# RWKV-6 attention with a SERF feed-forward: level six beside the state's products, and the last factor of the keys a step ahead

## The chip, the cores and the metric

The kernel runs on one core of one Trainium2 chip. The metric is the device time of one execution in microseconds (us). Five engines with their own queues work beside each other and meet by semaphores: TensorE (PE; its weight loads are shown apart as PEld), VectorE (DVE), ScalarE (ACT), GpSimd (POOL) and SyncE (SP), whose queue here only starts DMA transfers. All data is float32.

## The reference, cut to what matters

Attention with a decaying state, 4 batches, 8 heads, 768 tokens, head size 48; then a feed-forward on 3072 tokens (384 to 2048 to 384):

```python
for t in range(S):
    cur = einsum('bhd,bhe->bhde', u * k_t, v_t)
    y[:, :, t] = einsum('bhd,bhde->bhe', r_t, state + cur)
    state = w_t[..., None] * state + einsum('bhd,bhe->bhde', k_t, v_t)

h = x @ w_in
sp = maximum(h, 0.0) + log1p(exp(-abs(h)))     # softplus
g = h * erf(sp)
out = g @ w_out
```

`x` is `y` with heads and head size joined. The recurrence runs along the tokens, so the kernel can't treat them all at once.

## The kernel before, in words

**Steps.** The tokens are cut into chunks of 128, each into two halves of 64. A step is one chunk of a pair of batches, with all 8 heads: 12 steps, 0 to 11. Within a half, r and k are multiplied level by level with products of decays (levels one to six, blocks of 2 to 64 tokens), and small products of r and k give the attention inside the half (`own`). Across halves the state carries over (`middle` is the state between the two halves of a chunk, `S` before, `S_next` after).

**Late steps.** Steps 5 to 11 are written by `attend_late`. They take the nearest 16 tokens in another way: VectorE and GpSimd multiply rows of r, k and decays for each distance 1 to 15 (`term`, L463 and L467), VectorE sums them (L453), and the sums go through DRAM and back (`by_blocks`, `by_tokens`) to become the next step's `own` (L514). This preparation of step s + 1 is a generator, `prepare`, run in pieces (`next(following)`, the token F) inside step s. The same generator multiplies k by its decays in place; the result goes to DRAM (`k_blocks`, L499) and comes back with the tokens on the partitions as `kT` (L509). `kT` still lacks the decay over whole blocks of 16: `spread_blocks` turns `over_blocks` by two small products with the identity (L672), copies them (`few`, L678), sends them out (`g_rows`, L683) and fetches them repeated (`spread`, L688); VectorE multiplies `kT` by `spread` (L718). Products of `kT` and v give the state's increment (`state_part`, L659).

**Small products on TensorE.** All of these use 48 or 64 rows, and four or so at once in parts of the array: `from_own` (L584, own times v, into `y`), `level_products` (L552), `through_state` (L610, r times state), `state_part` (L659), the spread products (L672). Between them stand the large products of the feed-forward, 128 by 128.

**The feed-forward, by tokens.** A table, `LATE` and `USUAL`, says what is done in the seven stages of a late step. P is a piece of the projection of step s - 3 (8 products of 192 columns, `project_fast`, L1142; in steps before 6, four of 384, L1059), H a piece of the hidden layer of step s - 1 (6 products of 256 columns, L1027, and a ScalarE copy out of PSUM, L1036). Both write PSUM tiles named m, of which there are two: an H can start only when the tile before the last has been read. s is a softplus of a chunk of hidden values, e an erf into a PSUM lane (ey into the tile y, ep into pp1), m the multiplication of the chunk by its lane (VectorE, L992); every softplus and every erf loads its own ScalarE table first. k puts a quarter of the gated hidden values into a lane (L1100), S1 to S4 are the blends of a product scheme with seven factors (L1119 to L1125).

**Order.** A manual schedule: every engine executes in the order in which the program issues. PSUM has two tiles for the attention, pp0 and pp1; the lane p is pp1. In a late step TensorE's order is: `from_own` of the step before (swap 1) and level five; P; `from_own` (swap 0) and `through_state`; four P; level six and the spread products; two P; the state's products; eight H. VectorE begins with the fence (`seen`, L593), a small read of `y` that the second `from_own` waits for, then scales by level five (L328) and takes its products (L562); the near terms, the sums, kT's factor, level six's scale, the additions to an output (L1162, L1167, which free the tiles m that the last P wrote), the blends and the late sums follow; `own` ends its step. GpSimd multiplies the far terms in a step, then the products of decays and two fades of the state (L713, L739).

Of the kernel before, what the change touches and what calls it, by code (L numbers as in the profile page):

```python
# [11 lines left out]
FP32 = mybir.dt.float32  # L12
# [5 lines left out]
P = 128  # L18
FAST = 3
EP = 64  # L20
HC = 64
NC = 2
# [20 lines left out]
LOG = 6  # L43
# [18 lines left out]
def kernel(  # L62
# [47 lines left out]
    faded = [const.tile([P, JP, D], FP32, name="faded")] * NC  # L110
    seen = const.tile([P, NE * NP * NC], FP32, name="seen")

    over_blocks = const.tile([P, C // NEAR, JP], FP32, name="over_blocks")
    u_sb = const.tile([P, NP], FP32, name="u_sb")
    ident = const.tile([P, P], FP32, name="ident")
    mask_sb = const.tile([P, MASKED, HC], I32, name="mask_sb")
# [87 lines left out]
    def near_log(s):  # L204
        return NEAR_LOG - (s == DIRECT)
# [97 lines left out]
    def rows(e, n=D):  # L303
        return slice(e * EP, e * EP + n)
# [7 lines left out]
    def scale(s, level, batch=None):  # L312

        in_t, tots = loaded[s][0], ready[s][1]
        half, nb = 1 << (level - 1), JP * C >> level
        if batch is not None:
            nb //= NJ
            halves = view(
                turns["first"][:, batch], half, [[NP * C - half, 2], [2 * half, nb], [1, half]]
            )  # L320
            nc.vector.tensor_mul(
                halves, halves,
                view(tots[level - 1], 2 * batch * nb, [[1, 2], [2, nb], [0, half]]),
            )
# [3 lines left out]
        nc.vector.tensor_mul(  # L328
            halves, halves, view(tots[level - 1], 0, [[1, n], [2, nb], [0, half]])
        )  # L330
# [23 lines left out]
    def prepare(s):  # L354
# [61 lines left out]
        if s == DIRECT:  # L416
            yield
        else:
            half = view(tots[NEAR_LOG + 1], 1, [[2, NC], [C >> NEAR_LOG + 1, JP]])
            quarter, last = (  # L420
                view(tots[NEAR_LOG], n, [[4, NC], [C >> NEAR_LOG, JP]]) for n in (1, 3)
            )
            to = over_blocks[:].rearrange("p (h b) n -> p b h n", h=NC)
# [83 lines left out]
        if near == NEAR:  # L507
# [2 lines left out]
                out=kTs[s][:], in_=k_blocks[:].rearrange("(g b) s d -> (b s) g d", g=NH)  # L510
            )
        scale(s, near_log(s))
        nb = HC // NEAR
        nc.vector.tensor_mul(  # L514
            own[:].rearrange("p n (b t) -> p n b t", t=NEAR),
# [148 lines left out]
                        stop=True,  # L664
                    )

    def spread_blocks(s, pp):


        n = D // 2  # L670
        for e in range(NE):
            nc.tensor.matmul(  # L672
                pp[:EP, e, 0:2, HC // 2 : HC // 2 + n],
                lhsT=over_blocks[rows(e)].rearrange("p b n -> p (b n)"),
                rhs=ident[rows(e), rows(e)], start=True, stop=True,
            )
        few = att.tile([EP, NE * 2, n], FP32, name="few", bufs=1)
        nc.scalar.copy(  # L678
            few[:].rearrange("p (e i) d -> p e i d", e=NE),
            pp[:EP, :, 0:2, HC // 2 : HC // 2 + n],  # L680
        )
        g_rows = dram.tile([C // NEAR, JP * NE * D], FP32, name="g_rows")
        nc.sync.dma_start(  # L683
            out=g_rows[:].rearrange("b (n d) -> (b n) d", n=JP),
            in_=few[:].rearrange("p i d -> p (i d)"),
        )
        spread[s] = att.tile([P, JP, NE, D], FP32, name="spread", bufs=1)
        nc.sync.dma_start(  # L688
            out=spread[s][:].rearrange("p n e d -> p (n e d)"),
            in_=g_rows[:, None, :].to_broadcast([C // NEAR, NEAR, JP * NE * D]),  # L690
        )

    def attend_late(s, run):

        c, in_t, vt, own, S, S_next, ends = parts_of(s)
        RK = by_pair(in_t)
        before = s - 1 if s - 1 > DIRECT else None
        if before:
# [19 lines left out]
        nc.vector.tensor_mul(  # L718
            kT[:].rearrange("p (e n) d -> p n e d", e=NE),
            kT[:].rearrange("p (e n) d -> p n e d", e=NE), spread[s][:],  # L720
        )
# [24 lines left out]
    def attend_first(xT):  # L746

# [572 lines left out]
    def in_order(s, k):  # L1320
# [3 lines left out]
        for what in order[k]:  # L1324
# [8 lines left out]
    STAGES_LATE = ("front", "near", 0, 1, 2, 3, 4)  # L1333
    LATE = {
        DIRECT + 1: (
            "s ey", "m", "s ep m P P s ey m P P P", "s P F ep m P F P k22y k11p F", "S1",
            "S2 S3 H k12y S4 H F", "s H ep m H H F G s H H H ep",
        ),
        n_steps - 1: (
            "s P", "m w", "ey P m s P P ep P", "m P P", "", "", ""  # L1340
        ),
    }
# [70 lines left out]
    with tc.manual_schedule(  # L1413
# [15 lines left out]
        for s in range(n_steps):  # L1429
# [167 lines left out]
```

## Time and profile before

| what | value |
|---|---|
| runs | 586.53, 583.72, 584.1 us; median 584.1 |
| profiled execution | 586.88 us, its span 585.1 us |
| granted TensorE clock | 0.999 |
| one late step, 7 to 10 | 44.5 us (TensorE's first `from_own` at 285.73, 330.23, 374.73, 419.23 and 463.71) |
| in step 8 (330.2 to 374.7): busy | PE 44.50, DVE 40.26, ACT 29.32, POOL 27.83 us |

The profile is one execution. The time of an execution has 1.8 us in front of and behind the span. A line of a timeline gives the start from the span's beginning, the duration, engine, line of the program, operation, destination and sources, shape and count; in brackets the idle time before it and what ended that. Neighbouring instructions of one kind are merged: a matmul in float32 makes two records, so a group of 32 products shows 64. The ends of matmuls are modelled; distances from start to start are the safer reading. A small group shows its first record's start.

### The profile page before, as it was taken

To read this page: it belongs to the slowest core of one execution; us is meant where nothing else is said; L and a number is where in the kernel's file an instruction comes from. 1 tells how busy PE (TensorE), PEld (TensorE's weight loads), DVE (VectorE), ACT (ScalarE), POOL (GpSimd) and SP (SyncE) were. 2 spreads that over 40 slices of the span, in tenths; PEclk is the share of its full clock that TensorE was granted. 3 is DMA by queue.
4 is the path that set the end of the run, shared out by engine and by line. 5 is a ranking of instruction groups with operands and counts; after the bars stand their busy time and mean duration, and the time that the engine had idled before them with its cause. 6 is when DMAs were issued, how large, how long until landed. Compare 5 with 4: busy or idle time off the path is not lost.

```text
span 585.1 us, 16663 instructions
## 1 busy us (share of the span) xinstructions
PE 576.4 (99%) x7240; PEld 495.1 (85%) x7240; DVE 454.7 (78%) x558; ACT 355.6 (61%) x478; POOL 274.1 (47%) x313
## 2 busy tenths in 40 slices
PE   8899999999999999999999999999999999999997
PEld 6588887688668758998898898898898899988997
DVE  6776886999996899799799799799799637256630
ACT  3658877644544598756766666665765771387700
POOL 4557391702398469659459459449549200000000
PEclk9999999999999999999999999999999999999999
DMA  8587571440433414334334334334331301000000
GB/s 269 177 273 281 201 235 44 183 154 10 145 95 116 117 55 156 63 116 165 74 111 169 74 108 172 75 108 136 74 108 55 74 8 36 2 0 2 28 27 29
DMA packets 54082, 63.25 MB, mean 108 GB/s; under 512 B 35160, under 2 KB 40568, under 8 KB 52984
## 3 DMA queue, kind: packets, MB, share of 16 engines
q1 hardware_dynamic: 53624, 61.98, 33.4%
q8 instruction: 57, 0.93, 0.6%
q10 hardware_dynamic: 384, 0.20, 0.1%
q14 instruction: 17, 0.14, 0.1%
HBM read 52.39 MB, written 8.69 MB: 104 GB/s over the span
## 4 chain that ended last, share of the span: by engine, by line
PE 95%; DVE 3%; issue 1%; ACT 0%; POOL 0%; DVEq 0%; POOLq 0%
PE m L1027 36%; PE m L1142 28%; PE m L1059 8%; PE pp L552 6%; PE pp L1230 4%; PE y L1230 2%; PE y L584 2%; PE pp L659 2%; PE y L610 2%; PE m L862 1%; PE pp L871 1%; PE pp L938 1%; DVE in L328 1%; DVE words L467 1%; PE pp L1142 0%
## 5 line engine op out<-in xcount | busy, mean ns | idle before, releaser
L1027 PE MATMUL m<-xT,w_in_sb 128*128 128x256 f32 x960 | 215.3, 382 | 0.1
L1027 PEld LDWEIGHTS m<-xT,w_in_sb 128*128 128x128 f32 x960 | 179.9, 190 | 26.2 <-issue 1.0
L328 DVE TENSOR_TENSOR in<-in,tot_sb 128x1024 f32<-128x1024 f32 (+1 forms) x55 | 75.3, 1369 | 16.5 <-PE pp L552 13.2
L463 POOL TENSOR_TENSOR rk<-words 128x528 f32<-128x528 f32 (+3 forms) x28 | 42.5, 1517 | 91.2 <-DVE sums L453 80.7
L1036 ACT COPY h<-m 128x512 f32<-128x512 f32 x80 | 46.4, 579 | 57.6 <-PE m L1027 57.5
L467 POOL TENSOR_TENSOR words<-words,rest 128x528 f32<-128x528 f32 (+10 forms) x77 | 78.1, 1015 | 6.0
L1059 PE MATMUL m<-w_out_sb,h 128*128 128x384 f32 x192 | 64.3, 491 | 0.0
L1059 PEld LDWEIGHTS m<-w_out_sb,h 128*128 128x128 f32 x192 | 35.7, 190 | 23.5
L1142 PE MATMUL m<-mixed,h 128*128 128x192 f32 x256 | 45.6, 331 | 0.0
L1142 PE MATMUL m<-w_out_sb,h 128*128 128x192 f32 x256 | 44.8, 329 | 0.0
L552 PEld LDWEIGHTS pp<-in 48*64 48x64 f32 (+1 forms) x2368 | 33.4, 126 | 12.0 <-issue 6.2
L1142 PEld LDWEIGHTS m<-mixed,h 128*128 128x128 f32 x256 | 41.4, 190 | 0.9
L1142 PEld LDWEIGHTS m<-w_out_sb,h 128*128 128x128 f32 x256 | 41.6, 190 | 0.3
L1142 PE MATMUL m<-w_out_sb,room 128*128 128x192 f32 x240 | 41.5, 326 | 0.0
L983 ACT ACT_TABLE_LOAD x30 | 38.5, 1283 | 2.7 <-issue 2.2
L987 ACT ACT_TABLE_LOAD x30 | 38.5, 1283 | 1.5 <-DVE room L1125 1.1
L1142 PEld LDWEIGHTS m<-w_out_sb,room 128*128 128x128 f32 x240 | 39.4, 190 | 0.0
L402 POOL TENSOR_TENSOR tot_sb<-tot_sb 128x256 f32<-128x256 f32 (+4 forms) x50 | 36.2, 724 | 3.8
L552 PE MATMUL pp<-in 48*64 48x32 f32 (+1 forms) x2368 | 37.3, 212 | 0.6 <-DVE in L328 0.5
L463 POOL TENSOR_TENSOR words<-words 128x336 f32<-128x336 f32 (+6 forms) x49 | 35.3, 720 | 3.8
L453 DVE TENSOR_REDUCE sums<-rk 128x14 f32<-128x672 f32 (+9 forms) x54 | 34.7, 701 | 0.0
L453 DVE TENSOR_REDUCE sums<-words 128x6 f32<-128x288 f32 (+8 forms) x66 | 26.9, 464 | 3.9 <-POOL words L463 3.6
(198 smaller groups left out, 951.5 us busy)
## 6 DMA issues: line engine op xcount, KB each, us to landing
in<-in_rkw SPq DMA_DIRECT2D x8, 1024.0 KB, 5.1
words<-in_moe_w_in SPq DMA_DIRECT2D x16, 384.0 KB, 5.4
words<-in_moe_w_out SPq DMA_DIRECT2D x16, 384.0 KB, 4.7
words<-in_rk_rows SPq DMA_DIRECT2D x8, 768.0 KB, 5.6
w<-in_rkw SPq DMA_DIRECT2D x11, 512.0 KB
v<-in_v SPq DMA_DIRECT2D x12, 384.0 KB, 5.6
out<-o SPq DMA_DIRECT2D x23, 192.0 KB, 2.4
in<-in_rkw SPq DMA_DIRECT2D x7, 512.0 KB, 5.7
```

Source lines behind the costliest of these rows:

```text
L328: nc.vector.tensor_mul(halves, halves, view(tots[level - 1], 0, [[1, n], [2, nb], [0, half]]))
L402: nc.gpsimd.tensor_mul(new, pair[:, :, 0], pair[:, :, 1])
L453: nc.vector.tensor_reduce(out=view(sums[:], n, [[near * (NEAR + 1), NEAR // near], [NEAR + 1, near - n]]), in_=terms[n], axis=mybir.AxisLi ...
L463: engine.tensor_mul(terms[n], r[:, :, n:], k[:, :, : near - n])
L467: engine.tensor_mul(k[:, :, :m], k[:, :, :m], w[:, :, n : n + m])
L552: nc.tensor.matmul(to, lhsT=rk(1, n)[rows(e), s0 : s0 + m], rhs=right, start=True, stop=True,)
L983: nc.scalar.activation(sp_room, chunks[0], AF.Softplus)
L987: nc.scalar.activation(at, sp_room, AF.Erf)
L1027: nc.tensor.matmul(ps[:, ff, :], lhsT=w_in_sb[:, g * FG + f + ff, kk * P : (kk + 1) * P], rhs=xT[:, kk, :], start=kk == 0, stop=kk == KT - 1,)
L1036: nc.scalar.copy(h[:, f : f + FT, :], ps[:])
L1059: nc.tensor.matmul(ps[j][:], lhsT=gs[g][:, f, j * C : (j + 1) * C], rhs=w_out_sb[:, g * FG + f, :], start=g + f == 0, stop=g == NG - 1 and ...
L1142: nc.tensor.matmul(to, lhsT=a[:, f], rhs=b[:, f], start=start and f == 0, stop=f == FG - 1, skip_group_check=True,)
```

## The change

It concerns the late steps only, `attend_late` and what it calls.

- Level six's products come right after the second P, and the state's products follow them at once, into pp1 instead of pp0. The sums into `middle` and `S_next` follow the near terms on VectorE; the fade of `middle` is on VectorE instead of GpSimd.
- The two spread products become one product with all 128 rows. `over_blocks` gets a second half of ones so that the stationary side has 128 columns, of which 64 are used. It stands after the fifth P.
- `kT` is multiplied by `spread` at the end of the step before (`fade_keys`), behind a further piece of `prepare`: `own` is now its own last piece, behind the step's last chunk. Step 5 multiplies `kT` at its own beginning.
- The last chunk is multiplied at the step's end instead of in stage "near" of the next; in the tables one or two P move to "near". In step 5 the order of chunks and lanes changes: "ey", its m, then "ey" and "ep". One piece of weight joining moves from step 11 behind the last fence.

```diff
@@ prepare: over_blocks of two halves, a further yield ahead of own
-    over_blocks = const.tile([P, C // NEAR, JP], FP32, name="over_blocks")
+    over_blocks = const.tile([P, 2, C // NEAR, JP], FP32, name="over_blocks")
...
         scale(s, near_log(s))
+        yield
         nb = HC // NEAR
@@ spread_blocks
+        if s > DIRECT + 1:
+            got = products([P, NE * JP * HC], 0)[:, : NE * D].rearrange("p (e d) -> p e d", e=NE)
             nc.tensor.matmul(
-                pp[:EP, e, 0:2, HC // 2 : HC // 2 + n],
-                lhsT=over_blocks[rows(e)].rearrange("p b n -> p (b n)"),
-                rhs=ident[rows(e), rows(e)], start=True, stop=True,
+                got, lhsT=over_blocks[:].rearrange("p i b n -> p (i b n)"),
+                rhs=ident[:].rearrange("p (e m) -> p e m", e=NE)[:, :, :D],
+                start=True, stop=True,
             )
...
@@ attend_late
         take_level(own, pp, LOG - 1)
+        if s == DIRECT + 1:
+            fade_keys(s)
         run("front", None)
...
+        run("near", None)
+        pp = products([P, NE, JP, HC], 0)
+        level_products(pp, RK, LOG)
+        ps = products([P, NC, JP, HC], 1)
+        ps = [[ps[:, h]] * NE for h in range(NC)]
+        state_part(s, kTs[s], ps)
+        take_level(own, pp, LOG)
         following = prepare(s + 1) if s + 1 < n_steps else iter(())
         next(following, None)
         nc.gpsimd.tensor_mul(faded[0][:], S[:], ends[:, :, 0:1].to_broadcast([P, JP, D]))
         next(following, None)
-        run("near", None)
-        next(following, None)
-        kT = kTs[s]
-        nc.vector.tensor_mul(
-            kT[:].rearrange("p (e n) d -> p n e d", e=NE),
-            kT[:].rearrange("p (e n) d -> p n e d", e=NE), spread[s][:],
-        )
-        run(0, following)
-
-        pp = products([P, NE, JP, HC], 0)
-        level_products(pp, RK, LOG)
-        if s + 1 < n_steps:
-            spread_blocks(s + 1, pp)
-        take_level(own, pp, LOG)
-        scale(s, LOG)
-        run(1, following)
-        ps = products([P, NC, JP, HC], 0)
-        ps = [[ps[:, h]] * NE for h in range(NC)]
-        state_part(s, kT, ps)
-        run(2, following)
         for e in range(NE):
             nc.vector.tensor_add(middle[rows(e)], faded[0][rows(e)], ps[0][e][rows(e), :, :D])
-        run(3, following)
         if s < n_steps - SPC:
-            nc.gpsimd.tensor_mul(
+            nc.vector.tensor_mul(
                 faded[1][:], middle[:], ends[:, :, 1:2].to_broadcast([P, JP, D])
             )
             for e in range(NE):
                 nc.vector.tensor_add(S_next[rows(e)], faded[1][rows(e)], ps[1][e][rows(e), :, :D])
-        run(4, following)
+        next(following, None)
+        scale(s, LOG)
+        run(0, following)
+        if s + 1 < n_steps:
+            spread_blocks(s + 1)
+        for n in range(1, 5):
+            run(n, following)
+        for _ in following:
+            pass
+        if s + 1 < n_steps:
+            fade_keys(s + 1)
+
+    def fade_keys(s):
+
+        kT = kTs[s][:].rearrange("p (e n) d -> p n e d", e=NE)
+        nc.vector.tensor_mul(kT, kT, spread[s][:])
@@ the tables
     LATE = {
         DIRECT + 1: (
-            "s ey", "m", "s ep m P P s ey m P P P", "s P F ey m P F P k22y k11p F", "S1",
-            "S2 S3 H k12y S4 H F", "s H ep m H H F G s H H H ep",
+            "s ey", "m P P", "s ey m s ep m P P P", "s P F ey m P F P k11p k22y F", "S1",
+            "S2 S3 H k12y S4 H F", "s H ep m H H F G s H ep H H m F",
         ),
         n_steps - 1: (
-            "s P", "m w", "ey P m s P P ep P", "m P P", "", "", ""
+            "s P", "P", "ey m s P P ep P", "m P P", "", "", ""
         ),
     }
     USUAL = (
-        "s P", "m", "ey P m s P P ep P", "m k22y P F P k11p F F", "S1", "S2 S3 H k12y S4 H F",
-        "s H ey m H H F s H ep H H",
+        "s P", "P", "ey m s P P ep P", "m k22y P F P k11p F F", "S1", "S2 S3 H k12y S4 H F",
+        "s H ey m H H F s H ep H H m F",
     )
@@ the end
-        run_late(s - 1, "S Q w w w")
+        run_late(s - 1, "S Q w w w w")
```

More of the change, by code (lines that the diff above doesn't have):

```diff
@@ L422, in prepare @@
             )
-            to = over_blocks[:].rearrange("p (h b) n -> p b h n", h=NC)
+            to = over_blocks[:, 0].rearrange("p (h b) n -> p b h n", h=NC)
             nc.gpsimd.tensor_mul(to[:, 0], quarter, half)
@@ L665, in state_part, with spread_blocks @@
                     )
-    def spread_blocks(s, pp):
-        n = D // 2
-        for e in range(NE):
+    def spread_blocks(s, pp=None):
+        few = att.tile([EP, NE, D], FP32, name="few", bufs=1)
+        if s > DIRECT + 1:
+            got = products([P, NE * JP * HC], 0)[:, : NE * D].rearrange("p (e d) -> p e d", e=NE)
             nc.tensor.matmul(
-                pp[:EP, e, 0:2, HC // 2 : HC // 2 + n],
-                lhsT=over_blocks[rows(e)].rearrange("p b n -> p (b n)"),
-                rhs=ident[rows(e), rows(e)], start=True, stop=True,
-            )
[L677 to L680, printed above, removed]
-        )
+                got, lhsT=over_blocks[:].rearrange("p i b n -> p (i b n)"),
+                rhs=ident[:].rearrange("p (e m) -> p e m", e=NE)[:, :, :D],
+                start=True, stop=True,
+            )
+            nc.scalar.copy(few[:], got[:EP])
+        else:
+            n = D // 2
+            got = pp[:EP, :, 0:2, HC // 2 : HC // 2 + n]
+            for e in range(NE):
+                nc.tensor.matmul(
+                    got[:, e], lhsT=over_blocks[rows(e), 0].rearrange("p b n -> p (b n)"),
+                    rhs=ident[rows(e), rows(e)], start=True, stop=True,
+                )
+            nc.scalar.copy(few[:].rearrange("p e (i d) -> p e i d", i=2), got)
         g_rows = dram.tile([C // NEAR, JP * NE * D], FP32, name="g_rows")
@@ L684, in spread_blocks @@
             out=g_rows[:].rearrange("b (n d) -> (b n) d", n=JP),
-            in_=few[:].rearrange("p i d -> p (i d)"),
+            in_=few[:].rearrange("p e d -> p (e d)"),
         )
@@ L714, in attend_late @@
         next(following, None)
-        run("near", None)
-        next(following, None)
-        kT = kTs[s]
-        nc.vector.tensor_mul(
-            kT[:].rearrange("p (e n) d -> p n e d", e=NE),
-            kT[:].rearrange("p (e n) d -> p n e d", e=NE), spread[s][:],
-        )
-        run(0, following)
-        pp = products([P, NE, JP, HC], 0)
-        level_products(pp, RK, LOG)
-        if s + 1 < n_steps:
-            spread_blocks(s + 1, pp)
-        take_level(own, pp, LOG)
-        scale(s, LOG)
-        run(1, following)
-        ps = products([P, NC, JP, HC], 0)
-        ps = [[ps[:, h]] * NE for h in range(NC)]
-        state_part(s, kT, ps)
-        run(2, following)
         for e in range(NE):
             nc.vector.tensor_add(middle[rows(e)], faded[0][rows(e)], ps[0][e][rows(e), :, :D])
-        run(3, following)
         if s < n_steps - SPC:
-            nc.gpsimd.tensor_mul(
+            nc.vector.tensor_mul(
                 faded[1][:], middle[:], ends[:, :, 1:2].to_broadcast([P, JP, D])
@@ L1335 @@
         DIRECT + 1: (
-            "s ey", "m", "s ep m P P s ey m P P P", "s P F ep m P F P k22y k11p F", "S1",
-            "S2 S3 H k12y S4 H F", "s H ep m H H F G s H H H ep",
+            "s ey", "m P P", "s ey m s ep m P P P", "s P F ey m P F P k11p k22y F", "S1",
+            "S2 S3 H k12y S4 H F", "s H ep m H H F G s H ep H H m F",
         ),
         n_steps - 1: (
-            "s P", "m w", "ey P m s P P ep P", "m P P", "", "", ""
+            "s P", "P", "ey m s P P ep P", "m P P", "", "", ""
         ),
```

## The prediction

> **What bounds the kernel now.** I read the page first, then the timelines of the late steps, engine by engine. TensorE is busy for 99% of the span and carries 95% of the chain that ended last:
>
> ```profile
> PE 576.4 (99%) x7240; PEld 495.1 (85%) x7240; DVE 454.7 (78%) x558; ACT 355.6 (61%) x478; POOL 274.1 (47%) x313
> ...
> PE 95%; DVE 3%; issue 1%; ACT 0%; POOL 0%; DVEq 0%; POOLq 0%
> ```
>
> So there are two ways to move the end: shorten what TensorE does, or make it wait. The timeline of TensorE in step 8 (start us, duration, line, records; step 8 starts at 330.23, step 9 at 374.73, so a step is 44.50 us) shows its price list:
>
> ```profile
> 331.73 2.87 PE L1142 MATMUL m<-w_out_sb,h 128*128 128x192 f32 x16
> 334.52 0.67 PE L584 MATMUL y<-own,v 64*48 64x64 f32 x32
> ...
> 336.01 2.87 PE L1142 MATMUL m<-mixed,h 128*128 128x192 f32 x16
> 338.72 2.76 PE L1142 MATMUL m<-w_out_sb,room 128*128 128x192 f32 x16
> 341.32 2.76 PE L1142 MATMUL m<-mixed,room 128*128 128x192 f32 x16
> ...
> 346.61 0.76 PE L552 MATMUL pp<-in 48*32 48x32 f32 x64
> 347.30 0.32 PE L672 MATMUL pp<-ident,over_blocks 48*64 48x48 f32 x4
> 347.55 2.87 PE L1142 MATMUL m<-mixed,h 128*128 128x192 f32 x16
> ...
> 352.94 0.94 PE L659 MATMUL pp<-v,kT 64*48 64x48 f32 x64
> 353.81 20.99 PE L1027 MATMUL m<-xT,w_in_sb 128*128 128x256 f32 x96
> ```
>
> Start to start, a projection piece (P) between two others takes 2.60 us (338.72 to 341.32), one after a small group 2.71, one between two small groups 2.79 (331.73 to 334.52). A visit to the small products costs its neighbours 0.20. I call the first hidden piece (H) of a step H1; here it starts at 353.81, 23.58 into the step.
>
> VectorE, GpSimd and SyncE of step 8 (idle time and releaser in brackets):
>
> ```profile
> 331.87 1.22 DVE L328 TENSOR_TENSOR in<-in,tot_sb 128x1024 f32<-128x1024 f32 x1 [0.74 <-PE pp L552]
> ...
> 341.29 1.21 DVE L992 TENSOR_TENSOR h<-h,pp 128x1024 f32<-128x1024 f32 x1
> ...
> 347.22 1.72 DVE L718 TENSOR_TENSOR kT<-kT,spread 128x768 f32<-128x768 f32 x1
> ...
> 351.73 0.54 DVE L1162 TENSOR_TENSOR o<-o,m 128x384 f32<-128x384 f32 x1
> ...
> 372.93 1.51 DVE L514 TENSOR_TENSOR own<-block_sb,by_tokens 128x1024 f32<-128x1024 f32 x1 [1.62 <-DMA by_tokens<-by_blocks]
> ```
>
> ```profile
> 343.40 1.31 POOL L463 TENSOR_TENSOR rk<-words 128x528 f32<-128x528 f32 x1 [14.52 <-DVE sums L453]
> ...
> 366.69 0.28 POOL L467 TENSOR_TENSOR words<-words,rest 128x48 f32<-128x48 f32 x1
> ```
>
> ```profile
> 367.00 0.33 SPq L499 DMA_DIRECT2D k_blocks<-words  x1
> ...
> 370.21 0.99 SPq L509 DMA_DIRECT2D kT<-k_blocks  x1
> ```
>
> Here is a loop from step to step. X is the scaling of level five (L328, 331.87). From it VectorE needs 9.42 us to the end of the four near terms (341.29), 1.13 for a chunk, 0.98 to the first sum and GpSimd's start (343.40); GpSimd works 23.57 (to 366.97); k_blocks goes out, kT is fetched at 370.21; by_tokens releases own at 372.93; the fence and the next X stand behind own. VectorE idles only 3.7 us in a step.
>
> **The change part by part.**
>
> *Small groups.* Level six and the state's products become one group, so one visit less: 0.20. The two small spread products (0.25) become one full product of 96 columns, two records. Two bounds: 0.16 (2 x 96/192 of 0.1625 per record) and 0.28 (2 x 142 ns, the weight load of L938); its nearest rows are L938's, 0.93 us for 8 records of 128 columns, so 0.20. Saved 0.25 a step; a step without waits is 44.25. Steps 5 to 10 have it, six times: 1.5 us. In step 11 the state's products stood beside the next group already, so nothing is saved there.
>
> A rule weighed: the Trainium skill, TensorEngine Tiling (Array Packing), Key Properties, says that changing the tiling mode drains the array. That speaks against the fusion, for level six (48x32) and state (64x48) differ in shape and meet inside the new group. The trace has such a meeting: L552 takes 0.69 before L672 and 0.69 in step 11 before a full product, so one switch is exchanged for another. If the inner one came on top at a whole 0.20, the 1.5 us would be 0.3.
>
> *VectorE's order in a step.* The state's sums (two pairs, 1.14 and 1.15) and the fade of the middle (from GpSimd's 0.83 at L739; on VectorE 0.46 as L1162 to 0.83, I take 0.55 as a dependent operation) move in front of the first sum; one chunk (1.13) and kT's fade (1.64) leave that stretch. GpSimd therefore starts 13.24 after X, not 11.53.
>
> *kT times decays* moves to the end, behind own and before the fence. kT's DMA is issued at the same place as before; before, the fade came 17 us later than the fetch and nobody waited. Now: GpSimd's stretch loses the fade as a competitor (19.2 us would be its time at the uncontended rate of its last rows, 23.57 is measured; the fade is 1.64 of some 8 us of competing work): 22.7, between 22.4 and 23.57. Its end is X+35.9. kT lands 7.95 later (366.97 to 370.21, and 4.7):
>
> ```profile
> DMA to landing us min/median/max: 4.7/4.7/4.7
> ```
>
> X+43.9. The fade then takes 0.96 (step 11's row, GpSimd idle) to 1.72; with GpSimd done at about X+41.6 I take 1.0. Fence and start, 0.2: the next X is X+45.1 (44.8 to 46.6). That is longer than 44.25. Behind the waiting fade stand the fence, which the second from_own waits for 4.29 into the step, level five's scale, and at X+20.5 L1162, which must free the PSUM that H1 writes (before, 0 idle but 1.5 us to spare). So each step is drawn out to 45.1.
>
> A second rule: the Trainium skill, DMA: Bandwidth & Descriptors, Anatomy of one DMA, fits 2.0 us plus bytes/436e3 per us, on the software path. For 384 KB that would be 2.9 us where this trace has 4.7; then own, not kT, would be last, the period 44.2, and the result about 3.4 us lower.
>
> *ScalarE.* In the chunk lane pp, erf now has to wait for the state's sums, because they lie in pp1. In the usual steps ScalarE comes there 16.0 into the step and the sums are done at X+12.3, about 15.2: no wait. Level six itself comes 8.6 into the step; it needs level five's scale, done 3 to 5 in, and the state's products need kT, done before the fence: 4 us to spare in each. Level six's copies (1.16) now precede an erf and a softplus (4.59), so the copy that the fifth P needs ends about 0.2 after its place; hidden where the step waits anyway, 0.3 in step 11.
>
> *Step 5* is where it bites. Its rows before:
>
> ```profile
> 206.87 1.28 ACT L987 ACT_TABLE_LOAD   x1
> 208.17 1.03 ACT L987 ACTIVATE pp<-room 128x1024 f32<-128x1024 f32 x1
> ...
> 223.52 0.58 ACT L1036 COPY h<-m 128x512 f32<-128x512 f32 x1
> ```
>
> After: VectorE scales (197.29), takes level five, fades kT (to 200.3), then waits for the first erf (204.49) since the chunk m now stands ahead of the near terms: m to 205.66, terms 7.7 to 213.35, sums and fade 2.85 to 216.2. ScalarE stands at the pp erf from 212.6 to 216.2. Behind it are erf 2.3, few 0.13, softplus 2.3, the o copy 0.5, erf (waits for VectorE until 222.8) 2.3, o copy, two lane copies (the second waits for a chunk at 227.15): H1's copy ends at 228.7. Before it ended at 224.1. H3 cannot start before that: planned 225.3, so 3.4 lost. Then k12y waits for the blend, H2's copy 233.05 against H4's place: 1.75; later copies 0.6. Step 6 starts at 246.7, not 240.98: 5.7. GpSimd, started at 217.2, ends at 240.1; kT for step 6 lands 8.2 later at 248.3 and X is 249.6. TensorE comes to H1 of step 6 at 246.7 + 23.45, VectorE frees its PSUM at 249.6 + 20.6: both 270.2. No slack is left, and the loop's excess counts from there.
>
> *Tail.* One weight join (1.13) moves behind the last fence; VectorE was through with the tokens at 498.96 and is needed at 504.86: 0. GpSimd's larger over_blocks memset is at the start, beside loads: 0; without that cover, under 0.2. SyncE's g_rows waits for few, 5 us later in step 5; the loads behind it are used a step later: 0.
>
> *Sum.* Step 5: +5.7 (its 0.25 saved included). Four periods of 45.1 against 44.5, from H1 of step 6 to H1 of step 10: +2.4. Copies late in the last H phase and step 11's P: +0.4. Together +8.5. The sum is made in the profiled execution (586.88, of which 585.1 span), which would become 595.4; the three runs have the median 584.1 (583.72 to 586.53), so 592.6.
>
> **The rivals.**
>
> 1. *Not slower: nothing reaches TensorE.* -1.5: 582.6. It turns on one point: H1's copy in step 5 done by 225.2, for which the sums would have to end at about 212.7 instead of 216.2. Against it: each term is a measured row, and ScalarE's copies already trail by 0.9 there.
> 2. *Only step 5.* The loop closes within 44.25 (kT landing 0.9 sooner): 5.7 - 5 x 0.25 + 0.3 = +4.8: 588.9. For it: the excess is a small difference of large terms.
> 3. *A longer loop.* GpSimd's 23.57 unchanged and the fade at 1.4: 46.4, four times 1.3 more: 597.8.
> 4. *Clearly faster* needs 2.9 us, 0.5 a step; no row holds that.
>
> **How the numbers follow.** Main 46% (590.5 to 595.5), rival 1 14%, rival 2 20%, rival 3 16%, rival 4 4%. Half a per cent, about what a measurement here can tell, is 2.9 us: slower 0.82, same 0.14, faster 0.04. The range reaches from just under rival 2's lower edge to above rival 3: 584.5 to 600.5; rivals 1 and 4 are left out.
>
> **What would show it.** Right: TensorE idle in step 5 between 220 and 235, H1's copy at about 228; kT's fade waiting for a DMA at each step's end, at about 0.96; steps 6 to 10 near 45.1; three visits to small products. Wrong: step 6 starting at 241, steps of 44.25, or kT landed before own.

## The result, and the profile after

The changed kernel takes 594.57 us (median of 6 runs, 593.63 to 595.16); before took 585.32 us in 6 runs beside it (583.72 to 588.21). The ratio is 1.0152, with a 95% interval of 1.0122 to 1.0183: it is slower, by about 9.3 us. The prediction was 592.6 us, range 584.5 to 600.5.

The page of the profiled execution after (595.16 us, span 593.4 us; busy time per engine, then the shares of the chain that ended last):

```profile
PE 578.3 (97%) x7228; PEld 494.3 (83%) x7228; DVE 459.5 (77%) x563; ACT 355.9 (60%) x478; POOL 265.7 (45%) x308
...
PE 49%; DVE 8%; ACT 6%; issue 2%; DMA 1%; ACTq 0%; DVEq 0%
```

TensorE is still the busiest engine, but its share of the chain fell from 95% to 49%: now VectorE and ScalarE stand in the chain too. Cut at TensorE's own marks (the first level-five product of step 5, then the first `from_own` of each step), the two profiled executions compare like this:

| stretch | before, us | after, us | difference |
|---|---|---|---|
| start to step 5's level five | 196.14 | 194.31 | -1.83 |
| step 5 | 44.84 | 51.16 | +6.32 |
| step 6 | 44.75 | 45.77 | +1.02 |
| steps 7, 8, 9 | 44.50 each | 45.03, 45.03, 45.04 | +1.60 |
| step 10 | 44.48 | 44.89 | +0.41 |
| step 11 to the span's end | 121.39 | 122.17 | +0.78 |
| span | 585.1 | 593.4 | +8.3 |

The first row lies ahead of the first late step, and it varies from execution to execution (see the last section). From step 5 on, the changed kernel loses 10.13 us.

*Step 5.* TensorE's timeline of it after:

```profile
202.23 8.01 PE L1069 MATMUL m<-w_out_sb,h 128*128 128x384 f32 x24
210.08 0.36 PE L674 MATMUL pp<-ident,over_blocks 128*128 128x96 f32 x2
210.27 7.93 PE L1069 MATMUL m<-w_out_sb,h 128*128 128x384 f32 x24
219.66 2.86 PE L1037 MATMUL m<-xT,w_in_sb 128*128 128x256 f32 x12 [1.46 <-ACT o L1078]
224.58 5.45 PE L1037 MATMUL m<-xT,w_in_sb 128*128 128x256 f32 x24 [2.06 <-ACT o L1078]
231.81 13.73 PE L1037 MATMUL m<-xT,w_in_sb 128*128 128x256 f32 x60 [1.78 <-ACT h L1046]
245.47 0.66 PE L585 MATMUL y<-own,v 64*48 64x64 f32 x32
```

Three times TensorE stands still and waits for a ScalarE copy: ahead of H1 and H2 for the last outputs' copies, which free their PSUM tiles, and ahead of H4 for the copy of a hidden piece. VectorE's and ScalarE's rows of the same stretch say why these copies are late:

```profile
202.52 1.22 DVE L1002 TENSOR_TENSOR h<-h,y 128x1024 f32<-128x1024 f32 x1 [4.06 <-ACT y L997]
```

```profile
214.30 1.28 ACT L997 ACT_TABLE_LOAD   x1 [3.63 <-DVE s L738]
...
221.80 1.28 ACT L997 ACT_TABLE_LOAD   x1 [2.19 <-DVE h L1002]
...
226.36 0.58 ACT L1046 COPY h<-m 128x512 f32<-128x512 f32 x1
```

VectorE stands 4.06 us ahead of the chunk's product, so near terms and state's sums come late; ScalarE stands 3.63 us ahead of the erf into pp1 until these sums are done, and every copy behind it is late.

*A usual step.* TensorE in step 8 after (shortened to the places that changed):

```profile
336.27 0.66 PE L585 MATMUL y<-own,v 64*48 64x64 f32 x32
...
345.54 0.94 PE L660 MATMUL pp<-v,kT 64*48 64x48 f32 x64
346.40 2.87 PE L1152 MATMUL m<-w_out_sb,room 128*128 128x192 f32 x16
349.11 2.76 PE L1152 MATMUL m<-mixed,room 128*128 128x192 f32 x16
352.21 2.87 PE L1152 MATMUL m<-w_out_sb,room 128*128 128x192 f32 x16 [0.34 <-ACT o L1163]
354.91 0.36 PE L674 MATMUL pp<-ident,over_blocks 128*128 128x96 f32 x2
355.11 2.79 PE L1152 MATMUL m<-mixed,h 128*128 128x192 f32 x16
...
360.33 21.04 PE L1037 MATMUL m<-xT,w_in_sb 128*128 128x256 f32 x96
381.30 0.67 PE L585 MATMUL y<-own,v 64*48 64x64 f32 x32
```

The spread product costs 0.20 (354.91 to 355.11). The fifth P waits: start to start 3.10 us instead of 2.60 (349.11 to 352.21), and the piece that starts afresh behind the wait takes 2.70 instead of 2.60, about 0.6 in all. The phase H takes 20.97 us (360.33 to 381.30); in step 10, undisturbed, it takes 20.81 (450.42 to 471.23).

VectorE in the same step, whose end is the beginning of the next:

```profile
336.93 0.96 DVE L754 TENSOR_TENSOR kT<-kT,spread 128x768 f32<-128x768 f32 x1 [0.41 <-DMA kT<-k_blocks]
...
337.91 1.23 DVE L328 TENSOR_TENSOR in<-in,tot_sb 128x1024 f32<-128x1024 f32 x1
...
355.03 1.46 DVE L328 TENSOR_TENSOR in<-in,tot_sb 128x512 f32<-128x512 f32 x1
...
358.79 0.55 DVE L1172 TENSOR_TENSOR o<-o,m 128x384 f32<-128x384 f32 x1
...
364.81 1.21 DVE L1129 TENSOR_TENSOR room<-h,y 128x1024 f32<-128x1024 f32 x1
...
381.99 0.96 DVE L754 TENSOR_TENSOR kT<-kT,spread 128x768 f32<-128x768 f32 x1 [0.34 <-DMA kT<-k_blocks]
```

kT's fade waits for its DMA, as forecast, but for a few tenths only; X, the scaling of level five, is at 337.91, L1172 is the addition that frees the PSUM for H1, and 364.81 is the blend S1. GpSimd's first and last far term, the issue of kT's DMA, and ScalarE's lane copy k12y, which waits for S1, in the same step:

```profile
351.21 1.31 POOL L463 TENSOR_TENSOR rk<-words 128x528 f32<-128x528 f32 x1 [16.83 <-DVE sums L453]
...
373.81 0.28 POOL L467 TENSOR_TENSOR words<-words,rest 128x48 f32<-128x48 f32 x1
```

```profile
377.33 0.98 SPq L509 DMA_DIRECT2D kT<-k_blocks  x1
```

```profile
366.05 1.02 ACT L1110 COPY y<-h 128x1024 f32<-128x1024 f32 x1 [2.34 <-DVE room L1129]
```

### The profile page after: what moved, and what is told of

It reads as the page before. It is cut to its first block, busy times and chain, and to the rows that moved or that the text cites. A ratio compares the mean times of both kernels' runs of the same rounds, so it can differ in the third digit from the quotient of the medians.

```text
span 593.4 us, 16627 instructions
## 1 busy us (share of the span) xinstructions
PE 578.3 (97%) x7228; PEld 494.3 (83%) x7228; DVE 459.5 (77%) x563; ACT 355.9 (60%) x478; POOL 265.7 (45%) x308
## 4 chain that ended last, share of the span: by engine, by line
PE 49%; DVE 8%; ACT 6%; issue 2%; DMA 1%; ACTq 0%; DVEq 0%
PE m L1152 20%; PE m L1037 18%; PE pp L1240 4%; PE y L1240 2%; DVE in L328 2%; PE pp L553 1%; ACT L997 1%; ACT y L997 1%; PE y L585 1%; DVE sums L453 1%; ACT room L993 1%; ACT own L570 1%; PE y L611 1%; DVE words L467 1%; DVE rk L463 1%
## 5 line engine op out<-in xcount | busy, mean ns | idle before, releaser
L463 POOL TENSOR_TENSOR rk<-words 128x528 f32<-128x528 f32 (+3 forms) x28 | 39.4, 1406 | 107.7 <-DVE sums L453 97.2
L328 DVE TENSOR_TENSOR in<-in,tot_sb 128x1024 f32<-128x1024 f32 (+1 forms) x55 | 82.0, 1490 | 5.3 <-PE pp L553 3.0
L1152 PE MATMUL m<-mixed,h 128*128 128x192 f32 x256 | 45.1, 329 | 0.0
L1152 PE MATMUL m<-w_out_sb,room 128*128 128x192 f32 x240 | 42.7, 331 | 1.8 <-ACT o L1163 1.8
L1002 DVE TENSOR_TENSOR h<-h,pp 128x1024 f32<-128x1024 f32 x14 | 17.0, 1217 | 20.8 <-ACT pp L997 20.8
```

The costliest lines, as they stand in the source:

```text
L328: nc.vector.tensor_mul(halves, halves, view(tots[level - 1], 0, [[1, n], [2, nb], [0, half]]))
L463: engine.tensor_mul(terms[n], r[:, :, n:], k[:, :, : near - n])
L1152: nc.tensor.matmul(to, lhsT=a[:, f], rhs=b[:, f], start=start and f == 0, stop=f == FG - 1, skip_group_check=True,)
```

## The experiments

Three explanations for the 45.03 us of a usual step were put against each other. All lines are of the changed kernel.

- **Theory A**, the prediction's: X, near terms, GpSimd, kT's DMA, kT's fade, fence, next X. In the trace after, GpSimd starts at X + 13.3 (351.21) and is done at X + 36.2 (374.09), kT's DMA is issued 3.2 later (377.33) and lands after 4.7, at X + 44.1; then the fade and the fence, 0.96, so 45.04 (337.91 to 382.95). VectorE waits for that landing ahead of X in steps 7, 8 and 9 (0.34 to 0.41 us), so the time is all in the chain's own links.
- **Theory B**, read from the trace after: the fifth P waits for ScalarE's copy L1163, which now stands behind level six's copies, an erf and a softplus. With a step of 44.26 without waits that alone gives 44.87 to 44.89, what step 10 takes.
- **Theory C**, formed only after the first four experiments: TensorE's level five, X 1.65 after the step's start, VectorE's work to S1 (26.90), then ScalarE's lane copy k12y, which needs S1 and stands ahead of the copies of H, to TensorE's next step (16.49): 45.04. X starts 1.16 behind level five's first product in steps 7 to 9, just as in steps 6 to 11 before, where VectorE is seen waiting for TensorE at this place (0.74 us in step 8).

### Step 5 in the order of before

All other steps as changed. Step 5 gets the body that `attend_late` had before, with the two small spread products and kT's fade behind the near terms; kT for step 6 is faded at step 5's end.

```diff
+        if s == DIRECT + 1:
+            run("front", None)
+            following = prepare(s + 1)
...
+            spread_blocks(s + 1, pp)
...
+            fade_keys(s + 1)
+            return
-            "s ey", "m P P", "s ey m s ep m P P P", "s P F ey m P F P k11p k22y F", "S1",
+            "s ey", "m", "s ep m P P s ey m P P P", "s P F ep m P F P k22y k11p F", "S1",
```

> Step 5 alone goes back to the order of before (near terms ahead of the first chunk, level six behind five P, state's products in pp0, two spread products); kT of step 6 is still multiplied at its end, steps 6 to 11 stay as changed. If step 5's loss comes from the erf in lane pp that waits for the state's sums, step 5 (TensorE, level five to the next step's first own) takes about 45 us instead of 51.2, and the time is near 588.5 (594.6 less 6). Rival: the loss belongs to kT's late fade for step 6, which is left here: then step 5 or 6 keeps several us of it and the time stays above 591. Steps 7 to 10 should keep 44.9 to 45.05 under either theory.

Measured: 588.59 us (587.01 to 590.65), ratio 1.0056 (1.0033 to 1.0079). Step 5 takes 45.72 us (195.57 to 241.29) instead of 51.16, steps 7 to 9 stay at 45.01, 45.02 and 45.05. The change's loss therefore lies in two places: 5.4 us in the order of step 5 (6.0 between the medians, which hold the early steps too), the rest in the steps behind it, whose 45.03 doesn't depend on step 5. Step 5 is still 0.9 longer than before; no run took that apart.

### kT's fade behind the fence

The fade goes from the end of the step before to the place behind level five in its own step: kT's DMA has 2 us more, and the fence no longer waits for it.

```diff
-        if s == DIRECT + 1:
-            fade_keys(s)
+        fade_keys(s)
         run("front", None)
...
-        if s + 1 < n_steps:
-            fade_keys(s + 1)
```

> kT's fade moves from the end of the step before to behind the fence and level five of its own step (as step 5 has it); nothing else. Theory A, the loop VectorE - GpSimd - k_blocks - kT - fade - fence sets the 45.03 us of steps 7 to 10: the fence then waits for own only, by_tokens lands about 2 us before kT did, the loop is about 44.3 and the steps go to 44.3 to 44.4; the time falls by about 3 us against the changed kernel. Theory B, ScalarE's late copy ahead of the fifth P sets them (0.5 to 0.6 a step) and the loop only just keeps pace: the steps go to about 44.9 and the time falls by 0.5 to 0.8 us. Step 5 keeps about 51 under both.

Measured: 598.15 us (597.49 to 599.51), ratio 1.0234 (1.0211 to 1.0256): slower still. Steps 6 to 9 take 45.95, 45.89, 45.91 and 45.89 us. Neither A (44.3) nor B (44.9) allows that. TensorE in this run (the phase H of step 8 and the start of step 9):

```profile
371.03 13.73 PE L1034 MATMUL m<-xT,w_in_sb 128*128 128x256 f32 x60 [0.22 <-ACT h L1043]
384.69 0.66 PE L585 MATMUL y<-own,v 64*48 64x64 f32 x32
```

TensorE waits ahead of H4 for a copy of H. The fade's 0.87 us now stands between X and S1 (27.77 us instead of 26.90), and the step is longer by just these 0.87. That is what led to theory C: 1.65 + 27.77 + 16.49 = 45.91.

### Level six's ScalarE copies later

The copies of level six (L570) go behind the erf, the softplus and two P, so that L1163 isn't behind them.

```diff
-        take_level(own, pp, LOG)
+        turns["six"] = lambda: take_level(own, pp, LOG)
+        if s == DIRECT + 1:
+            turns.pop("six")()
...
-        "s P", "P", "ey m s P P ep P", "m k22y P F P k11p F F", "S1", "S2 S3 H k12y S4 H F",
+        "s P", "P", "ey m s P P t ep P", "m k22y P F P k11p F F", "S1", "S2 S3 H k12y S4 H F",
...
+            elif what == "t":
+                turns.pop("six")()
```

> Level six's two copies on ScalarE are issued behind the erf, the softplus and the copies of two P in steps 6 to 11, so the copy that the fifth P waits for comes 1.2 us sooner; kT's fade stays at the step's end. Theory A (the loop): the wait ahead of the fifth P goes, but the steps stay at 45.0, with TensorE waiting later in the step, at the hidden pieces; the time stays within 0.5 us of the changed kernel. Theory B (the copy): steps of 44.4, the time 3 us lower.

Measured: 593.78 us (593.28 to 594.16), ratio 1.0155 (1.0136 to 1.0174). The wait at the fifth P is gone, and yet steps 7 to 9 take 45.03, 45.06 and 45.06 us. Only step 10 falls, from 44.89 to 44.26. So B is real (step 10 shows its 0.63), but with B gone something else takes exactly its place. TensorE and ScalarE in step 8:

```profile
359.47 21.66 PE L1039 MATMUL m<-xT,w_in_sb 128*128 128x256 f32 x96
381.06 0.66 PE L585 MATMUL y<-own,v 64*48 64x64 f32 x32
```

```profile
372.45 1.26 ACT L1048 COPY h<-m 128x512 f32<-128x512 f32 x2
```

The phase H is 21.59 us instead of 20.81: the 0.6 moved from the fifth P into H, where two copies come one right behind the other, late.

### Both of these together

The edits of the two experiments before, kT's fade behind the fence and the copies later, in one kernel.

> The edits of the last two together. Both theories: steps 7 to 10 at 44.3 to 44.4, the time 3 to 3.5 us under the changed kernel, step 5 still 51. If the steps stay above 44.7, a third wait holds them, most likely the late S1 blend and the lane copy ahead of the second hidden piece's copy.

Measured: 596.37 us (596.04 to 599.48), ratio 1.0212 (1.0181 to 1.0243). Steps 7 to 9 take 45.90, 45.90 and 45.88 us, step 10 takes 44.26. With A's fade out of its loop and B's copy out of the way there is still a period of 45.9. A third limit exists; the interval X to S1 is 27.77 in step 8 of both runs that have 45.9, and 26.89 to 26.91 there in the three that have 45.03 (the changed kernel and the two runs whose fade is left at the step's end). TensorE also stands about 0.36 ahead of H1 in steps 7 to 9 here, for the addition behind the moved fade; kT's DMA has no part in that, since X is 1.16 behind level five.

### Levels two and three behind S1

Theory C's own test: VectorE's two operations for levels two and three, 3.5 us, leave the stretch between X and S1.

```diff
-        "s P", "P", "ey m s P P ep P", "m k22y P F P k11p F F", "S1", "S2 S3 H k12y S4 H F",
+        "s P", "P", "ey m s P P ep P", "m k22y P F P k11p", "S1 F F", "S2 S3 H k12y S4 H F",
```

> The changed kernel with one move in steps 6 to 10: VectorE's two operations for levels two and three (L328, 3.5 us together) go from ahead of the blend S1 to right behind it. Nothing is added or removed. Theory C (the period is the loop TensorE's level five -> VectorE -> S1 -> ScalarE's copies -> the pieces H -> next step; 1.65 + 26.90 + 16.49 = 45.04): this loop falls by up to 3.5 us and no longer binds; what is left is TensorE's own 44.27 and the wait of about 0.6 ahead of the fifth P, so steps 7 to 9 take 44.85 to 44.9 and the kernel about 593.8 us (593.0 to 594.6). Theory A (the period is the loop from VectorE's level five over GpSimd and kT's transfer to kT's fade, 45.0): steps 7 to 9 stay at 45.03, and the kernel at 594.5.

Measured: 594.9 us (593.22 to 595.26), ratio 1.0165 (1.0146 to 1.0184), no difference from the changed kernel. Steps 7 to 9 take 44.95, 45.06 and 44.95 us: neither the 44.87 of C nor 45.03 throughout. C is removed here and next to nothing is gained. By its time the run did not decide; its trace speaks for A right behind C: X now stands 2.09 to 2.21 behind level five's first product instead of 1.16, so it no longer waits for TensorE, while kT's fade waits 0.55 to 0.71 for its DMA.

### Levels two and three behind S1, and the copies later

B and C both out; only A's path is as the changed kernel has it.

> The move of levels two and three behind S1 together with the move of ScalarE's level-six copies behind the erf, the softplus and two P: both the loop over S1 and the wait ahead of the fifth P are gone, kT's path alone is left as the changed kernel has it. Theory C: no other loop binds, steps 7 to 10 take 44.3 us instead of 45.0, and the kernel about 591.5 us (590.5 to 592.5). Theory A: kT's path is 45.0 by itself; as soon as VectorE's level five has lost what it has to spare (it drifts by 0.7 us a step against TensorE), steps take 45.0 again, and the kernel stays above 593.

Measured: 593.25 us (592.0 to 594.74), ratio 1.0143 (1.0122 to 1.0165). Steps 7 to 10 take 45.11, 44.98, 45.16 and 44.27 us. So A binds by itself. TensorE and VectorE in step 8:

```profile
360.28 20.99 PE L1039 MATMUL m<-xT,w_in_sb 128*128 128x256 f32 x96 [0.44 <-DVE o L1174]
381.20 0.67 PE L585 MATMUL y<-own,v 64*48 64x64 f32 x32
```

```profile
338.82 1.22 DVE L328 TENSOR_TENSOR in<-in,tot_sb 128x1024 f32<-128x1024 f32 x1
...
359.68 0.55 DVE L1174 TENSOR_TENSOR o<-o,m 128x384 f32<-128x384 f32 x1
...
382.85 0.96 DVE L756 TENSOR_TENSOR kT<-kT,spread 128x768 f32<-128x768 f32 x1 [0.64 <-DMA kT<-k_blocks]
...
383.81 1.22 DVE L328 TENSOR_TENSOR in<-in,tot_sb 128x1024 f32<-128x1024 f32 x1
```

X to X is 44.99 us (338.82 to 383.81), VectorE waits 0.64 for kT's DMA, and TensorE waits 0.44 ahead of H1 for the addition that frees its PSUM. This is the place the prediction named. X stands 2.60 after the step's start, not 1.65: the loop had to use up that slack before it could hold TensorE. In step 10 the state's last sums and the fade are left out of VectorE's order, the loop is shorter, and the step takes 44.27.

### Step 5's first chunk behind the near terms

The other part of the loss, with one move in the changed kernel: the table of step 5 gets an eighth stage, "terms", run between the near terms and the state's sums.

```diff
-            "s ey", "m P P", "s ey m s ep m P P P", "s P F ey m P F P k11p k22y F", "S1",
-            "S2 S3 H k12y S4 H F", "s H ep m H H F G s H ep H H m F",
+            "s ey", "P P", "s ey m s ep m P P P", "s P F ey m P F P k11p k22y F", "S1",
+            "S2 S3 H k12y S4 H F", "s H ep m H H F G s H ep H H m F", "m",
...
         next(following, None)
+        if s == DIRECT + 1:
+            run("terms", None)
         for e in range(NE):
```

> The changed kernel with one move in step 5 alone: the step's first chunk product m on VectorE, which stood 4.06 us waiting for ScalarE's erf ahead of the near terms, is called behind the near terms' first part and ahead of the state's sums. Theory of step 5 (the step is long because VectorE stands at m, so the near terms and the state's sums are late, ScalarE stands at its lane until these sums are done, and H1's copy comes 13 us late for TensorE): the sums come about 4 us earlier and step 5 takes 47.3 us (46.8 to 48) instead of 51.2, the kernel 590.6 us (589.8 to 591.6). Rival (step 5 is long because of its order on TensorE, level six and the state's products ahead of everything): step 5 stays at 51 and the kernel at 594.5.

Measured: 590.42 us (589.77 to 591.99), ratio 1.009 (1.0071 to 1.0109). Step 5 takes 47.04 us (194.36 to 241.40). VectorE's product and TensorE's phase H in this run:

```profile
206.12 1.21 DVE L1004 TENSOR_TENSOR h<-h,y 128x1024 f32<-128x1024 f32 x1
```

```profile
218.09 7.93 PE L1039 MATMUL m<-xT,w_in_sb 128*128 128x256 f32 x36
227.73 13.74 PE L1039 MATMUL m<-xT,w_in_sb 128*128 128x256 f32 x60 [1.71 <-ACT h L1048]
```

The product no longer waits, the two waits ahead of H1 and H2 are gone, and step 5 is 4.1 us shorter, the 4.06 of VectorE's stand. The new order of TensorE in step 5 stayed; that rival falls. Step 6, though, takes 46.64 us instead of 45.77, so 3.2 us come back between the two profiled executions (4.15 between the medians). kT's fade for step 6 waits 0.95 for its DMA and takes 1.55, X is late, and TensorE stands ahead of H1 for VectorE's addition, at the place the prediction named:

```profile
266.14 8.04 PE L1039 MATMUL m<-xT,w_in_sb 128*128 128x256 f32 x36 [0.64 <-DVE o L1174]
```

### Everything named so far mended

The three groups of small products stay; step 5 is in the old order, kT's fade behind the fence, level six's copies late, levels two and three behind S1, and the sixth P with its addition to an output ahead of the second m.

```diff
-        "s P", "P", "ey m s P P ep P", "m k22y P F P k11p F F", "S1", "S2 S3 H k12y S4 H F",
+        "s P", "P", "ey m s P P t ep P", "P m k22y F P k11p", "S1 F F", "S2 S3 H k12y S4 H F",
```

> The three groups of small products kept, and everything mended that the runs so far named: step 5 in the order of before; kT's fade behind the fence in its own step; level six's copies on ScalarE behind the erf, the softplus and two P; levels two and three on VectorE behind S1; and the fourth P's addition ahead of the second m. By the sum: step 5 45.5 us, steps 6 to 10 44.3 us each (TensorE without waits) instead of 44.5 before, so 584.5 us (583.5 to 586), within 0.3% of before. If another loop binds at 45 all the same, 588.

Measured: 586.12 us (585.05 to 586.95), ratio 1.0017 (1.0005 to 1.0029). Step 5 takes 44.90 us, step 6 takes 45.44, steps 7 to 9 take 44.81, 44.79 and 44.79, step 10 takes 44.26. Half a microsecond was still missing in each of steps 7 to 9. ScalarE and TensorE in step 9:

```profile
407.92 1.28 ACT L1029 ACT_TABLE_LOAD   x1 [1.49 <-DVE room L1167]
...
410.18 1.18 ACT L1078 COPY h<-m 128x512 f32<-128x512 f32 x2
```

```profile
397.45 21.39 PE L1069 MATMUL m<-xT,w_in_sb 128*128 128x256 f32 x96
418.78 0.67 PE L585 MATMUL y<-own,v 64*48 64x64 f32 x32
```

Theory C's loop has a second branch: an erf waits 1.49 us for S4 (L1167), which the moved operations had pushed back; two copies of H come at once and the phase H takes 21.33 us.

### The same, with levels two and three behind all four blends

```diff
-        "s P", "P", "ey m s P P t ep P", "P m k22y F P k11p", "S1 F F", "S2 S3 H k12y S4 H F",
+        "s P", "P", "ey m s P P t ep P", "P m k22y F P k11p", "S1", "S2 S3 H k12y S4 F F H F",
```

> The version with everything mended, with one correction: VectorE's two operations for levels two and three go behind all four blends (S4), and not between S1 and S2. There, in steps 7 to 9, ScalarE stood 1.5 us ahead of an erf that waits for S4, two of H's copies came one behind the other, and the phase H took 21.33 us instead of 20.81. Expected: the phase H at 20.8 in steps 7 to 9, these steps at 44.3 us instead of 44.8, and the kernel 1.5 us below the version before it: 584.6 us (583.6 to 585.6), against 585.1 before, so no difference that can be measured. If the steps stay at 44.8, something else in the phase H holds TensorE, and the time stays at 586.

Measured: 584.92 us (583.17 to 586.06), ratio 0.9992 (0.9973 to 1.001). TensorE in step 9:

```profile
372.85 0.66 PE L585 MATMUL y<-own,v 64*48 64x64 f32 x32
...
396.31 21.10 PE L1069 MATMUL m<-xT,w_in_sb 128*128 128x256 f32 x96
417.34 0.66 PE L585 MATMUL y<-own,v 64*48 64x64 f32 x32
```

Steps 7 to 9 take 44.44, 44.44 and 44.49 us, step 10 takes 44.26; step 5 takes 44.77 and step 6 takes 44.89. The time is that of before within what can be told: what the change lost is back once these places are mended together. Its gain in the small products is worth at most 0.25 us a step, and some of it the phase H (21.03 us in step 9 against 20.81) still gives back. No version that beats before by a measurable amount was found.

## Why the prediction was right, and where it was not

**The size.** Forecast +8.5 us on the profiled execution, measured +8.3 in the span. But two misses offset each other: from step 5 on the loss was 10.13, 1.6 more than the sum said, and the profiled execution was 1.83 us ahead before the change begins, which no term of the sum covers. That the two totals lie 0.2 us apart is luck. The medians differ by 9.25; the forecast of 592.6 stood on a before of 584.1, and the one measured beside the change took 585.32.

**Step 5: right, by the named mechanism.** Forecast +5.7, measured +6.32. With the 1.83 us of the earlier steps added, the rows come out where the working put them: state's sums done at 216.03 (214.20 + 1.83; forecast 216.2), H1's copy done at 228.77 (226.94 + 1.83; forecast 228.7). Step 6 starts at 247.30 instead of 246.7. One link was off: the forecast let TensorE stop first at H3, while it already stops at H1 and H2, for the outputs' copies L1078, which hang behind the same ScalarE queue. Taking away VectorE's stand made step 5 4.1 us shorter, and the old order 5.4.

**Small groups: right.** A step without waits was to take 44.25; it takes 44.26 in step 10 of the runs without the wait at the fifth P. The spread product takes 0.20, as taken. The trace shows the whole 0.25 a step, and level six takes 0.69 ahead of the state's products (344.85 to 345.54 in step 8) as it did ahead of the spread products, so no price for a switch inside the new group shows. The rule that was weighed against it (the Trainium skill, TensorEngine Tiling (Array Packing), Key Properties: a change of the tiling mode drains the array) names no price.

**The period: the right number, the mechanism only one of three.** Forecast 45.1 from kT's path; measured 45.03; for steps 6 to 9 the sum had +2.4, and they took +2.62 (from step start to step start). The terms came out close: GpSimd's start at X + 13.3 (13.24), its stretch 22.9 (22.7), the fade 0.96 (1.0), and kT's landing 4.7 (4.7). The estimate of 2.9 us, worked out from the fit that the Trainium skill (DMA: Bandwidth & Descriptors, Anatomy of one DMA) gives for the software path, does not describe this transfer from SyncE's queue. Two slips of the working changed nothing: its upper bound of 46.6 adds up to 46.7, and kT's fade (347.22) stood behind GpSimd's start before (343.40), so it could not leave the stretch ahead of it. In steps 7 to 9 this loop holds TensorE at H1 only where nothing else binds (levels two and three behind S1, copies later), at 45.0; in step 6 it is also seen there when step 5's first chunk goes behind the near terms (0.64). In the changed kernel TensorE never stands at H1 in steps 7 to 9: L1172 is done there about 1 us ahead of it (359.34 against 360.33), although that addition ends at X + 21.4 and not at the forecast X + 20.5. H1 itself is late there, for the fifth P. The step that failed is "so each step is drawn out to 45.1": it took the loop that was found for the only one. What the runs showed in its place are three limits within 0.2 us of each other, 44.87 (B), 45.0 (A) and 45.04 (C), of which each hides the next. That the number 45.1 was met all the same is partly luck: C, which the working didn't have, gives the same step within some hundredths.

**ScalarE's copy ahead of the fifth P: mis-sized.** The working said "about 0.2 after its place; hidden where the step waits anyway, 0.3 in step 11". It costs about 0.6 with the fresh start. Where A or C holds the step, it takes up their slack and adds nothing; in steps 10 and 11, where neither does, it counts whole: 0.63 in step 10 (44.89 to 44.26 with the copies later), and in step 11 the fifth P starts 3.11 behind the fourth (484.06 to 487.17) instead of 2.60. So the stretch behind step 9, put at +0.4, was +1.19.

**Not in the prediction: X to S1.** Level six's scale was moved at no price. From its start to that of the next VectorE operation it took 0.60 us before (350.00 to 350.60) and takes 1.49 after (355.03 to 356.52). The fade of the middle and the four sums came into the stretch, a chunk and kT's fade left it, which nearly cancels. Together X to S1 grew from 25.84 (331.87 to 357.71) to 26.90. That is what closes theory C's loop at 45.04; with the 25.84 of before the same sum gives 44.0 (1.65 + 25.84 + 16.49), under the 44.26 of a step without waits.

**The rivals.** *Not slower* and *clearly faster* fell on step 5. *Only step 5* was disproved by steps of 45.03 with step 5 mended. *A longer loop* fell on its own terms: GpSimd's stretch is 22.9 and not 23.57, the fade 0.96 and not 1.4, and the steps take 45.03 and not 46.4.

## What to carry to other kernels

A tuned step can be held by several loops of nearly the same length, and a forecast that finds one of them can get the time right and the cure wrong: with one or two of the loops taken out the kernel took 593.25 to 598.15 us here, with all of them and step 5 mended 584.92. So list, for every engine, each chain that returns to itself a step later, with its length, and test them together as well as alone. An operation that moves past an in-order queue is paid by whoever stands behind it: one VectorE product that waited 4.06 us for an erf made TensorE's step 4.1 us longer, by way of ScalarE's queue.

## What was not expected of the hardware

**One operation, two prices, by where it meets GpSimd.** Level six's scale (L328, half width) beside GpSimd's far terms. Before, VectorE's row and GpSimd's rows around it:

```profile
350.00 0.68 DVE L328 TENSOR_TENSOR in<-in,tot_sb 128x512 f32<-128x512 f32 x1
```

```profile
348.20 1.80 POOL L467 TENSOR_TENSOR words<-words,rest 128x480 f32<-128x480 f32 x1
350.09 1.55 POOL L463 TENSOR_TENSOR rk<-words 128x432 f32<-128x432 f32 x1
```

After, GpSimd's rows around VectorE's L328 of 355.03, which is shown above with 1.46:

```profile
354.71 1.22 POOL L463 TENSOR_TENSOR rk<-words 128x480 f32<-128x480 f32 x1
356.01 1.54 POOL L467 TENSOR_TENSOR words<-words,rest 128x480 f32<-128x480 f32 x1
357.63 1.11 POOL L463 TENSOR_TENSOR rk<-words 128x432 f32<-128x432 f32 x1
```

GpSimd works beside it in both kernels. Before, VectorE starts at the moment a GpSimd operation ends (350.00), takes 0.68, and it is GpSimd's next one that grows (1.55 for what takes 1.11 at 357.63). After, VectorE starts 0.32 into a GpSimd operation that ends at 355.93; 1.46 is the rest of that, 0.90, and 0.56 of its own. Since GpSimd starts from VectorE's sums, the two meet in the same way in every step: L328 takes 0.68 in each of steps 6 to 10 before, and 1.45 or 1.46 in each of them after; in step 11, where GpSimd has nothing left to do, it takes 0.69 in both kernels. VectorE's chunk products, one of whose operands lies in PSUM, keep 1.21 to 1.22 beside GpSimd. The Trainium skill, SBUF — State Buffer, section "SBUF: two separate sides", says that the two engines share a pair of ports which one of them locks for a whole instruction when a VectorE operation has two operands in SBUF; these rows agree. So this operation, when it was moved, would have had to be priced by the GpSimd operation it was to meet, not by its own row.

**The steps ahead of the change vary.** Level five of step 5 starts at 196.14 us before and at 194.31 after, and between 193.24 and 195.57 in the first four experiments, which do the same up to there as the changed kernel. That is 2.3 us among equal beginnings, more than some of the differences that the experiments were to tell apart; the lengths of steps 7 to 9, read inside one execution, agree to some hundredths. Why the early steps vary was not looked into.
